# Two linear-attention blocks on one core: the denominators of six units summed through memory on VectorE

## The chip, the cores and the metric

The kernel runs on one core of a Trainium2 chip. The metric is device time in microseconds, the median of several executions. TensorE (PE) multiplies matrices, VectorE (DVE) and ScalarE (ACT) work elementwise, GpSimd (POOL) and SyncE (SP) issue most DMAs. Each engine works through its own instructions in program order and waits on semaphores for the others.

## The reference

Two independent blocks A and B, each with its own input and weights, and their outputs side by side. One block, with S = 2048 tokens, D = 640, 32 heads of 20:

```python
qkv = (x @ wqkv) -> q, k, v per head
phi = lambda t: where(t > 0, t + 1, exp(t)) + 1e-6
pq, pk = phi(q), phi(k)
kv  = einsum("bhsd,bhse->bhde", pk, v)
z   = einsum("bhsd->bhd", pk)
num = einsum("bhqd,bhde->bhqe", pq, kv)
den = einsum("bhqd,bhd->bhq", pq, z)[..., None] + 1e-6
o   = num / den
return concat_heads(o) @ wo
```

## The kernel before

All data is float32; matrices are multiplied as a high and a low half (three products each: high by high, high by low, low by high), rounded by ScalarE with the rest taken by VectorE.

The first half, up to about 290 us, projects the keys of both blocks, applies phi and gathers the products of phi(k) with the input. Its instructions are ordered by a planner (classes Plan and Job, method emit): each piece of work is noted with an engine, a cost and what it reads and writes, and the planner emits them engine by engine by their due times.

The second half has its order written out by hand. The queries are worked on in 8 units of 512 tokens, 0 to 3 of A and 4 to 7 of B. Features are laid out with the head in the fastest place, so that each of the five chunks of 128 partitions holds 4 dimensions of all 32 heads, and a partition belongs to head (partition mod 32). For each unit u there is

- a projection "q" (qmm, lines 890 to 892): five chunks c of 15 matmuls of 512 columns, going through five blocks k of the input, each block as a rounded high half xqh and a low half xql; then phi (qphi, lines 1058 to 1060), and the sum over chunks of phi(q) times z into a tile acc (qacc, lines 1068 and 1070), which holds for each of 128 partitions a partial denominator: four partitions per head still have to be added;
- an output stage "o" (outmm, line 1169): 14 steps, 7 products for each of two halves of the tokens, into the banks pa, pe and psb, evicted by ScalarE (line 1184) and VectorE (line 1185).

The output stage of a unit comes one projection late: q(u), then o(u - 1), then q(u + 1). Smaller work is hung into slots: ("q", u, c, k) is run after block k of chunk c of the projection, ("o", u, s) after step s of the output stage, and what hangs in one slot is issued in the order in which it was put there (functions at and run). A low half is issued on VectorE at the next slot or by flush. Of interest here, for unit v, with w = v - 1:

- load_xraw(v + 1, c) in q(v), chunk 3, and load_xq(v + 1, c) in q(v), chunk 4: the loads (SyncE) of the next unit's input, tile xqs (line 921) and its stored low half xql (line 925);
- round_xq(v + 1, c) in o(w), steps 4, 6, 8, 10 and 12: the five roundings on ScalarE (line 928) that the projection q(v + 1) needs one after the other;
- load_w of B's query weights in q(3), and split_w of them in o(2), steps 1, 3, 5, 7 and 9 (tiles wst, wh, wl); loads of the output stage's forms (form_load, line 1034) in o(3) and after; form_split and form_store, which make B's forms;
- the chain of unit v, in o(w) and on: split_acc makes a high and a low half of acc, denmm multiplies each with a matrix "same" of zeros and ones that adds the four partitions of a head and leaves the sum in all four (bank psd, lines 1080 and 1081), recip (line 1086) inverts in two halves, divide (line 1092) multiplies phi(q) with the inverse, and then d_sums, a_split and d_split make the operands of o(v).

The stage buffers (tag wst, 7 of them) are shared by turns among xqs, the weight loads and the sums of the forms; a load on SyncE waits until the turn's earlier user is done, and so does all that stands behind it on SyncE.

## Time and profile before

| | |
|---|---|
| median of 3 runs | 574.31 us (573.58 to 575.03) |
| profiled execution | 573.32 us |
| its span | 571.5 us |
| TensorE busy | 567.1 us, 99% |
| VectorE, ScalarE, GpSimd busy | 431.0, 341.7, 57.2 us |
| chain that ended last: TensorE, DMA, ScalarE, VectorE | 95%, 2%, 2%, 1% |
| output stages o(0) to o(6) begin at | 335.89, 369.37, 402.73, 436.09, 469.45, 502.81, 536.17 us |

The span is the profile's, from the first to the last instruction of the program. Matmuls overlap in TensorE, so that a group's mean duration is longer than the time that it adds; the chain counts that time.

### The profile page before, as it was taken

To read this page: it belongs to the slowest core of one execution; us is meant where nothing else is said; L and a number is where in the kernel's file an instruction comes from. 1 tells how busy PE (TensorE), PEld (TensorE's weight loads), DVE (VectorE), ACT (ScalarE), POOL (GpSimd) and SP (SyncE) were. 2 spreads that over 40 slices of the span, in tenths; PEclk is the share of its full clock that TensorE was granted. 3 is DMA by queue.
4 is the path that set the end of the run, shared out by engine and by line. 5 is a ranking of instruction groups with operands and counts; after the bars stand their busy time and mean duration, and the time that the engine had idled before them with its cause. 6 is when DMAs were issued, how large, how long until landed. Compare 5 with 4: busy or idle time off the path is not lost.

```text
span 571.5 us, 9524 instructions
## 1 busy us (share of the span) xinstructions
PE 567.1 (99%) x3544; PEld 537.5 (94%) x3544; DVE 431.0 (75%) x700; ACT 341.7 (60%) x619; POOL 57.2 (10%) x93
## 2 busy tenths in 40 slices
PE   9999999999999999999999999999999999999997
PEld 7999999999999999999998899898989989898997
DVE  6888687599887887976355699967788786758792
ACT  6877566673787767655246665746556464644541
POOL 0210011110010011110000103120012201001010
PEclk9999999999999999999999999999999999999999
DMA  8994765748858999686987986662363996122022
GB/s 294 391 249 126 178 168 138 207 139 253 265 152 228 273 293 265 192 250 201 248 243 242 335 275 219 232 211 106 115 232 134 349 391 241 46 75 93 0 93 93
DMA packets 68002, 117.61 MB, mean 206 GB/s; under 512 B 6516, under 2 KB 29812, under 8 KB 67956
## 3 DMA queue, kind: packets, MB, share of 16 engines
q1 hardware_dynamic: 59060, 89.94, 48.4%
q0 software_dynamic: 8608, 26.88, 16.9%
q8 instruction: 28, 0.46, 0.3%
q10 hardware_dynamic: 288, 0.20, 0.1%
q14 instruction: 18, 0.15, 0.1%
HBM read 71.11 MB, written 35.39 MB: 186 GB/s over the span
## 4 chain that ended last, share of the span: by engine, by line
PE 95%; DMA 2%; ACT 2%; DVE 1%; issue 0%; ACTq 0%; DVEq 0%
PE psg L299 23%; PE pa L1169 12%; PE ka L299 9%; PE psq L890 8%; PE psq L892 8%; PE psq L891 8%; PE pe L1169 6%; PE ke L299 5%; PE psk L689 4%; PE psb L1169 4%; PE kb L299 3%; DMA md<-mev 1%; PE pskv L537 1%; PE pskv L950 1%; DMA xj<-in_A_xt 1%; PE psm L564 1%
## 5 line engine op out<-in xcount | busy, mean ns | idle before, releaser
L299 PE MATMUL psg<-pkh,xnh 128*128 128x320 f32 x320 | 99.0, 309 | 0.0
L299 PE MATMUL psg<-pkl,xnh 128*128 128x320 f32 x320 | 98.8, 309 | 0.0
L299 PE MATMUL psg<-pkh,xnl 128*128 128x320 f32 x320 | 98.7, 308 | 0.0
L890 PE MATMUL psq<-xqh,wh 128*128 128x512 f32 x200 | 78.7, 393 | 0.0
L892 PE MATMUL psq<-xqh,wl 128*128 128x512 f32 x200 | 78.1, 391 | 0.0
L891 PE MATMUL psq<-xql,wh 128*128 128x512 f32 x200 | 77.9, 390 | 0.0
L299 PEld LDWEIGHTS psg<-pkl,xnh 128*128 128x128 f32 x320 | 60.1, 188 | 0.0
L299 PEld LDWEIGHTS psg<-pkh,xnl 128*128 128x128 f32 x320 | 60.1, 188 | 0.0
L299 PEld LDWEIGHTS psg<-pkh,xnh 128*128 128x128 f32 x320 | 60.0, 188 | 0.0
L470 ACT ACTIVATE kt<-ka 128x320 f32<-128x320 f32 x52 | 22.7, 437 | 53.6 <-PE ka L299 51.3
L1184 ACT ACTIVATE o<-pa 128x320 f32<-128x320 f32 x64 | 27.9, 438 | 44.8 <-PE pa L1169 44.6
L1060 DVE SCALAR_TENSOR_TENSOR pq<-eq,rq 128x512 f32<-128x512 f32 x40 | 27.6, 691 | 30.8 <-ACT rq L1059 29.9
L387 POOL DMA_DIRECT2D zacc<-ek x32 | 26.4, 832 | 243.7 <-DVE ek L480 187.8
L518 DVE TENSOR_TENSOR gacc<-psg,gacc 128x320 f32<-128x320 f32 x60 | 29.2, 489 | 28.0 <-PE psg L299 27.1
L1058 ACT ACTIVATE eq<-psq 128x512 f32<-128x512 f32 x40 | 23.9, 598 | 36.6 <-PE psq L892 34.2
L892 PEld LDWEIGHTS psq<-xqh,wl 128*128 128x128 f32 x200 | 37.5, 188 | 8.0
L891 PEld LDWEIGHTS psq<-xql,wh 128*128 128x128 f32 x200 | 37.6, 188 | 7.3
L890 PEld LDWEIGHTS psq<-xqh,wh 128*128 128x128 f32 x200 | 37.6, 188 | 7.2
L382 ACT ACTIVATE pkh<-ek,epst 128x640 fp32r<-128x640 f32 x32 | 26.5, 829 | 7.9 <-DVE ek L480 7.7
L1169 PE MATMUL pa<-fh,dah 128*128 128x320 f32 x96 | 29.7, 309 | 0.0
L1169 PE MATMUL pa<-fl,dah 128*128 128x320 f32 x96 | 29.6, 309 | 0.0
L1169 PE MATMUL pa<-fh,dal 128*128 128x320 f32 x96 | 29.6, 308 | 0.0
(212 smaller groups left out, 1553.8 us busy)
## 6 DMA issues: line engine op xcount, KB each, us to landing
zacc<-ek POOLq DMA_DIRECT2D x32, 320.0 KB, 5.7
xql<-xd SPq DMA_DIRECT2D x40, 256.0 KB, 4.6
xd<-xl SPq DMA_DIRECT2D x29, 320.0 KB, 5.1
out<-o POOLq DMA_DIRECT2D x28, 320.0 KB, 3.4
xns<-in_A_x SPq DMA_DIRECT2D x16, 320.0 KB, 4.7
xts<-in_B_xt_tiles SPq DMA_DIRECT2D x16, 320.0 KB, 4.6
xns<-in_B_x SPq DMA_DIRECT2D x16, 320.0 KB, 6.7
xqs<-in_A_xt SPq DMA_DIRECT2D x20, 256.0 KB, 4.9
```

What stands on the lines that cost most here:

```text
L299: nc.tensor.matmul(o, a.r, w.r, start=start and k == i == 0, stop=k == n - 1 and i == 2, skip_group_check=True)
L382: note("ACT", n + 110, lambda: act(hi.r, p.f, AF.Identity, bias=epst), [hi], [p, K0.all], by=8.0)
L387: note("POOL", 1.0, lambda: nc.gpsimd.dma_start(z.f, p.f, **kw), [z], [p], dma=1.0 if first else 1.86)
L518: tt(o, BK[k].tile[:, :HF], o, op=OP.add)
L689: nc.tensor.matmul(o[h][:, :HF], x[a].r, w[c][h * HF:h * HF + HF].r, start=c == 0 and i == 0, stop=c == NC - 1 and i == 2, skip_group_chec ...
L890: nc.tensor.matmul(o, whi, xhi, start=first, stop=False)
L891: nc.tensor.matmul(o, whi, xlo, start=False, stop=False)
L892: nc.tensor.matmul(o, wlo, xhi, start=False, stop=last)
L1058: nc.scalar.activation(e, ps, AF.Exp)
L1060: nc.vector.scalar_tensor_tensor(pq[u][:, c, :], e, 1.0, r, op0=OP.min, op1=OP.add)
L1169: nc.tensor.matmul(ps, x, y, start=start and n == i == 0, stop=n == len(terms) - 1 and i == 2, skip_group_check=True)
L1184: copy = lambda x, y: nc.scalar.activation(x, y, AF.Copy)
```

## The change

For the units 1 to 6 split_acc, denmm and recip are replaced. acc_out writes acc to memory (DRAM) with one DMA from SyncE; acc_turn reads it back with four DMAs, each into 32 partitions, so that the partition is a head and one of four groups of 128 tokens, and the four partial sums lie beside each other in the free dimension; acc_add adds them on VectorE (256 columns, then 128) and inverts 128 columns; spread copies the inverse to the four partitions of each head, 16 copies of 32 partitions by 128 columns, the groups 0 and 1 on ScalarE and 2 and 3 on VectorE. For units 2 to 6 acc_out and acc_turn hang in step 2 of o(v - 1), acc_add and the first spreads in step 9, the others in step 10, the two divisions in 11 and 12; for unit 1 all of these one step later. Units 0 and 7 keep the old chain. The planner gets a further argument, safe, of 0.0 where none is given; no call in the kernel gives one.

```diff
--- before.py
+++ after.py
@@ -83,7 +83,7 @@
         self.jobs = []
         self.pe_at = 0.0
 
-    def note(self, engine, n, fn, w, r, ahead=None, dma=None, late=None, by=None, due=None):
+    def note(self, engine, n, fn, w, r, ahead=None, dma=None, late=None, by=None, due=None, safe=0.0):
         base = self.RATE.get(engine)
         j = Job(engine, base[0] + base[1] * n if base else n, fn, ahead, dma)
         for part, writes in [(p, True) for p in w] + [(p, False) for p in r]:
@@ -106,7 +106,7 @@
         j.late = self.pe_at + (25.0 if late is None else late)
         if by is not None:
             j.late = self.pe_at + by
-        j.by, j.set = by, due
+        j.by, j.set, j.safe = by, due, safe
         self.jobs.append(j)
         return j
 
@@ -150,9 +150,21 @@
                     if e == "HOST":
                         if any(d.done is None for d in j.deps):
                             continue
-                    elif any(d.done is None or d.done + (LAG if d.engine != e or d.dma else 0) > now + 1e-9
-                             for d in j.deps):
-                        continue
+                    else:
+                        at = 0.0
+                        for d in j.deps:
+                            if d.done is None:
+                                at = None
+                                break
+                            t = d.done + (LAG if d.engine != e or d.dma else 0)
+                            if d.dma and j.safe:
+                                t += max(0.0, min(j.safe, j.due - t))
+                            at = max(at, t)
+                        if at is None:
+                            continue
+                        if at > now + 1e-9:
+                            events.add(at)
+                            continue
                     if j.ahead is not None and e != "PE" and j.due - j.ahead > now:
                         events.add(j.due - j.ahead)
                         continue
@@ -1034,6 +1046,7 @@
             nc.sync.dma_start(f32(t)[:, cs], d)
 
     pq, acc, den, dd = {}, {}, {}, {}
+    ad = {u: dram.tile([P, 512], F32, name=f"ad{u}") for u in range(1, NU - 1)}
 
     def qmm(u, c):
         b = u // NG
@@ -1080,6 +1093,36 @@
         nc.tensor.matmul(ps, same, t[:, 0], start=True, stop=False)
         nc.tensor.matmul(ps, same, t[:, 1], start=False, stop=True)
         den[u] = (ps, q2[0].tile([P, 512], F32, name="rd", tag="rd", bufs=1))
+
+    def acc_out(u):
+        nc.sync.dma_start(ad[u], acc[u])
+        den[u] = (None, q2[0].tile([P, 512], F32, name="rd", tag="rd", bufs=1))
+
+    def acc_turn(u):
+
+        v = ad[u].rearrange("(k h) (q j) -> q h k j", k=4, q=4)
+        for q in range(4):
+            nc.sync.dma_start(acc[u][q * H:q * H + H].rearrange("p (k j) -> p k j", k=4), v[q])
+
+    def acc_add(u):
+        t = acc[u]
+        nc.vector.tensor_tensor(t[:, :256], t[:, :256], t[:, 256:], op=OP.add)
+        nc.vector.tensor_tensor(t[:, :P], t[:, :P], t[:, P:256], op=OP.add)
+        nc.vector.reciprocal(t[:, :P], t[:, :P])
+
+    def spread(u, g, copy):
+
+        t = acc[u][g * H:g * H + H, :P]
+        for k in range(4):
+            copy(den[u][1][k * H:k * H + H, g * P:g * P + P], t)
+        if g == 3:
+            acc.pop(u)
+
+    def spread_a(u, g):
+        spread(u, g, lambda y, x: nc.scalar.activation(y, x, AF.Copy))
+
+    def spread_v(u, g):
+        spread(u, g, nc.vector.tensor_copy)
 
     def recip(u, h):
         ps, r = den[u]
@@ -1288,18 +1331,15 @@
                         (("o", v, 0), a_split, v, 0, 1), (("o", w, 13), d_sums, v, 0, 1),
                         (("o", v, 0), d_split, v, 0, 1), (("o", v, 2), d_sums, v, 1, 1),
                         (("o", v, 2), a_split, v, 1, 1), (("o", v, 3), d_split, v, 1, 1)]
-        elif v == 1:
-            chain[v] = [(("o", w, 4), split_acc, v), (("o", w, 7), denmm, v), (("o", w, 8), recip, v, 0),
-                        (("o", w, 10), recip, v, 1), (("o", w, 11), divide, v, 0),
-                         (("o", w, 12), divide, v, 1), (("q", u, 0, 2), d_sums, v, 0), (("q", u, 0, 4), a_split, v, 0),
-                         (("q", u, 1, 2), d_sums, v, 1), (("q", u, 2, 1), d_split, v, 0), (("q", u, 3, 1), a_split, v, 1),
-                         (("q", u, 3, 4), d_split, v, 1)]
         else:
-            chain[v] = [(("o", w, 2), split_acc, v), (("o", w, 5), denmm, v), (("o", w, 7), recip, v, 0),
-                        (("o", w, 9), recip, v, 1), (("o", w, 11), divide, v, 0),
-                         (("o", w, 12), divide, v, 1), (("q", u, 0, 2), d_sums, v, 0), (("q", u, 0, 4), a_split, v, 0),
-                         (("q", u, 1, 2), d_sums, v, 1), (("q", u, 2, 1), d_split, v, 0), (("q", u, 3, 1), a_split, v, 1),
-                         (("q", u, 3, 4), d_split, v, 1)]
+            o = 1 if v == 1 else 0
+            chain[v] = [(("o", w, 2 + o), acc_out, v), (("o", w, 2 + o), acc_turn, v), (("o", w, 9 + o), acc_add, v),
+                        (("o", w, 9 + o), spread_a, v, 0), (("o", w, 9 + o), spread_v, v, 2),
+                        (("o", w, 10 + o), spread_a, v, 1), (("o", w, 10 + o), spread_v, v, 3),
+                        (("o", w, 11 + o), divide, v, 0), (("o", w, 12 + o), divide, v, 1),
+                        (("q", u, 0, 2), d_sums, v, 0), (("q", u, 0, 4), a_split, v, 0),
+                        (("q", u, 1, 2), d_sums, v, 1), (("q", u, 2, 1), d_split, v, 0), (("q", u, 3, 1), a_split, v, 1),
+                        (("q", u, 3, 4), d_split, v, 1)]
     for v in range(NU):
         for a, f, *x in chain[v]:
             at(a, f, *x)
```

## The prediction

> **What bounds the kernel now.** I read the page first, then the chain that ended last, then the queue that issues the loads, then VectorE and ScalarE in the stages that the change touches. Busy time by engine and the chain, from the page:

> ```profile
> PE 567.1 (99%) x3544; PEld 537.5 (94%) x3544; DVE 431.0 (75%) x700; ACT 341.7 (60%) x619; POOL 57.2 (10%) x93
> PE 95%; DMA 2%; ACT 2%; DVE 1%; issue 0%; ACTq 0%; DVEq 0%
> ```

> TensorE works 99% of the span and is 95% of the chain (its granted clock is 1.00 in the rows by stretch further down). So a matmul taken out is time gained, and any wait put ahead of a matmul is time lost. The chain in order of time (start, length, what) shows two output stages; the first belongs to unit 2 and handles the denominators of unit 3, the second to unit 3 and those of unit 4:

> ```profile
> 402.73 1.76 PE pa L1169 x12
> ...
> 408.01 0.23 PE psd L1080
> 408.24 0.23 PE psd L1081
> 408.48 2.64 PE psb L1169 x18
> ...
> 419.03 0.23 PE psq L890
> ...
> 421.12 0.23 PE psq L890
> 421.80 0.23 PE psq L890
> ...
> 436.09 1.76 PE pa L1169 x12
> ...
> 455.16 0.23 PE psq L890
> ```

> The reader is to see that the pieces touch: no gap stands between the output stage and the projection behind it. I count time within a stage from its first row, T = 402.73 and T = 436.09. The stage with its two psd matmuls lasts 16.3 us.

> The third thing to see is the issue queue of SyncE. It works in program order and often stands at a load whose buffer is not free. Its DMAs in these two stages (start, time until the last of them is issued, count at the end):

> ```profile
> 408.20 0.92 SPq L925 DMA_DIRECT2D xql<-xd  x2
> 411.12 0.59 SPq L910 DMA_DIRECT2D wst<-in_B_wq  x1
> 411.80 1.49 SPq L925 DMA_DIRECT2D xql<-xd  x3
> 413.34 0.90 SPq L910 DMA_DIRECT2D wst<-md  x2
> ...
> 441.39 0.33 SPq L921 DMA_DIRECT2D xqs<-in_B_xt  x1
> 441.81 3.00 SPq L925 DMA_DIRECT2D xql<-xd  x5
> 444.91 0.67 SPq L1034 DMA_DIRECT2D fh<-fdh  x1
> ```

> **What goes.** Six units lose two matmuls of 512 columns, 0.23 us each on the chain: 6 x 2 x 0.23 = 2.8 us, all on the path. Their two weight loads overlap and count nothing. VectorE loses two reciprocals and the low half of a split, ScalarE the high half. Neither engine is the bound, so these are cover and not gain. One PSUM bank is used less, and the two "sr" buffers have one user fewer; no wait in the rows is for either, so I take zero for both. The new argument of the planner has the value 0 everywhere, so the first half of the kernel keeps its order: zero.

> **What comes, by price.** The rows for it, by line (count, busy us, mean ns):

> ```profile
> L1086 DVE RECIPROCAL rd<-psd 128x256 f32<-128x256 f32 x16 | 27.9, 1747 | 0.9 <-PE psd L1081 0.9
> L994 DVE TENSOR_TENSOR t<-wst 128x320 f32<-128x320 f32 x2 | 1.0, 488 | 0.0
> L954 DVE TENSOR_TENSOR kvt<-pskv,mask 120x120 f32<-120x120 f32 (+1 forms) x6 | 1.6, 265 | 2.3 <-PE pskv L950 2.3
> L884 ACT ACTIVATE kvh<-kvt 120x120 fp32r<-120x120 f32 (+1 forms) x6 | 1.7, 290 | 8.2 <-DVE kvt L954 8.2
> out<-o SPq DMA_DIRECT2D x2, 160.0 KB, 1.8
> DMA to landing us min/median/max: 2.6/4.6/6.4
> ```

> On VectorE: an add of 256 columns, between 0.27 and 0.49, say 0.42; one of 128, 0.27; a reciprocal of 128, half of 1.75, 0.88. Together 1.6 us. Four spreading copies per group on VectorE or ScalarE, 0.27 to 0.29 each with their overlap taken off, about 1.0 us a group. Per unit VectorE gives up 2 x 1.75 + 0.7 and takes 1.6 + 2.0: less work. ScalarE takes 2.0 and gives up 0.6; at 60% busy that is hidden if it comes on time.

> The DMAs are what matters: one of 256 KB out, then, only when it has landed, four of 64 KB back, each issued by SyncE in about 0.4 us. No row has 64 KB in blocks of 512 bytes to 32 partitions. Its bounds are the 1.8 us of a 160 KB transfer on an empty queue and the 4.6 us median of 256 KB (the last row above, for xql). I take 1.8, since SyncE has issued nothing else behind the first hop and so the queue has drained. From the landing of the first hop to that of the last return is then 3 x 0.4 + 1.8 = 3.0 us.

> **Where it stands in the queue.** The first hop is noted at step 2 of the output stage, but on SyncE it stands behind everything that the projection before noted: all five xql loads and, in T = 402.73, the last weight load of B. That one (411.12) waits for a buffer that VectorE frees at 411.1, after the psb addition:

> ```profile
> 409.84 0.49 DVE L1185 TENSOR_TENSOR o<-psb,o 128x320 f32<-128x320 f32 x1 [2.05 <-PE psb L1169]
> 410.27 0.82 DVE L881 TENSOR_TENSOR wl<-wst,wh 128x640 fp32r<-128x640 f32 x1
> ...
> 412.48 0.44 ACT L1184 ACTIVATE o<-pa 128x320 f32<-128x320 f32 x1 [2.22 <-PE pa L1169]
> 412.81 0.62 ACT L928 ACTIVATE xqh<-xqs 128x512 fp32r<-128x512 f32 x1
> ```

> So the first hop takes the place of the wst<-md at 413.34, 0.47 earlier by the missing matmuls: 412.9, which is T+10.1. The addition of the quarters is placed at step 9, which ends on TensorE about there. The landings in these places, from the DMA view of each of the two stretches:

> ```profile
> xql<-xd SPq DMA_DIRECT2D x3, 256.0 KB, 4.2
> wst<-md SPq DMA_DIRECT2D x2, 320.0 KB, 4.6
> ...
> xql<-xd SPq DMA_DIRECT2D x5, 256.0 KB, 6.3
> ```

> **Unit 3, step by step.** First hop issued 412.9, landed 4.4 later (between the 4.2 and 4.6 of its neighbours): 417.3. Returns landed 420.4. VectorE adds and inverts until 422.0. ScalarE, which has stood at its first spread since step 9, does four copies, the eviction of step 10 (0.33) and the rounding of the fourth xq block (0.62): 424.0. Then four copies, an eviction, and the fifth block: 426.0. Behind these waits are queued on VectorE the last wl, two divisions and two additions, on ScalarE those two roundings. The last wl comes out at about 424, before TensorE asks for it. TensorE asks for the fifth block at 421.80 - 0.47 = 421.3. It stands 4.7 us, at the fourth block and the fifth.

> **Unit 4.** The xqs load at 441.39 waits for a split on VectorE that comes about 1.3 us sooner, since the two halves of the old split no longer stand ahead of it. The hop takes the place of the fh at 444.91: 443.6. There the queue is full and xql takes 6.3: landed 449.9. Returns 452.9, added 454.6, fifth block rounded 4.0 later, 458.6. TensorE asks at 455.16 - 0.47 = 454.7: it stands 3.9 us. Behind this hop stand the twenty form loads for the next output stage; they start some 7 us later and that stage 3.4 later. The last of them is issued at 463.8 and goes into the sixth product of the stage that begins at 469.45, near 480, so this is covered.

> **The other four** are in time. The rows: the starts of the output stages of units 0, 1 and 4 from the chain, the last addition into the sums of units 1 and 2 from VectorE's timeline, and from SyncE's the last form load and the loads ahead of unit 5's hop.

> ```profile
> 335.89 1.76 PE pa L1169 x12
> ...
> 369.37 1.76 PE pa L1169 x12
> ...
> 469.45 1.76 PE pa L1169 x12
> ```

> ```profile
> 341.46 0.75 DVE L1070 SCALAR_TENSOR_TENSOR acc<-pq,z,acc 128x512 f32<-128x512 f32 x1
> 371.50 0.75 DVE L1070 SCALAR_TENSOR_TENSOR acc<-pq,z,acc 128x512 f32<-128x512 f32 x1
> ```

> ```profile
> 463.82 0.42 SPq L1034 DMA_DIRECT2D fl<-fdl  x1
> ...
> 468.76 2.61 SPq L925 DMA_DIRECT2D xql<-xd  x5
> ```

> The fifth block is asked for at T+18.6 (421.3 - 402.73), so the last return is due at 18.6 - 4.0 - 1.6 = T+13.0. In unit 2 the sums are ready at 372.25, T+2.9, with SyncE free: at most 2.9 + 4.6 + 3.0 = T+10.5, and I put unit 6 with it. Unit 5's loads have left SyncE by 471.4, T+1.9, so its hop too goes at T+2.9; the queue ahead is full, T+10.7. Unit 1, placed one step later, has its sums at 342.2, T+6.3; with the 2.6 us of a quiet queue and 3.0 it lands near T+12.0, against a deadline of T+13.9, because the fourth rounding stands ahead of its spread. A stall here would have no cover and count whole. The divisions come 2 to 3 us later everywhere; their products are wanted a whole projection later.

> **Sum.** -2.8 + 4.7 + 3.9 = +5.8 us. The profiled run took 573.32 (span 571.5), 1.0 below the median of 574.31; on the median the sum gives 580.1.

> **Rivals.**
> A. The first hop lands at the fastest xql time, 2.6, in both places. Unit 3 stalls 4.7 - 1.8 = 2.9, unit 4 3.9 - 3.7 = 0.2: +0.3, 574.6, no change. Against it: in the stretches concerned nothing landed so fast, and the DMA engines are nearly full:

> ```profile
> 412.50:418.00 5.50, 5.50 (x40) 5.50 (x39) 5.50 (x7) 3.80 (x8) 1.08 (x2) 1.00 0.95 331
> 441.00:451.00 10.00, 10.00 (x69) 9.91 (x68) 6.72 (x9) 5.03 (x11) 2.96 (x6) 1.00 0.85 277
> ```

> (DMA share is the last number but one: 0.95 and 0.85.) [...] The 4.2 to 6.3 us in these places speak against it here.
> B. The returns are slow, 4.6 each: 2.8 more in units 3 and 4, and past the deadlines by 0.9, 0.3, 0.5 and 0.3 in units 1, 2, 5 and 6: +13.4, 587.7. Only the missing row speaks for it.
> C. Faster: no stall, all 2.8 kept, 571.5. It needs the returns by T+13.0 in units 3 and 4 too, so the first hop issued by T+5.6 (4.4 and 3.0 ahead of it). It decides if SyncE is past its loads by then. Against it: 411.12 and 441.39 are waits for VectorE in this very stage, and the five xql follow them.

> **How the numbers follow.** The forecast, with its own range 577 to 584, gets 0.62; A 0.14, B and what lies between 0.12, C 0.09, beyond all 0.03. The range 573 to 588 leaves out C and the rest, 0.12. A measurement can tell about 0.3% (1.7 us) from no change. Faster 0.10 (C and the edge of A), same 0.10, slower 0.80.

> **What would show it.** In the changed profile psd should be left with 4 matmuls. Gaps on TensorE ahead of the fourth and fifth group of the first projection after the output stages of units 2 and 3, and nowhere else; VectorE idle ahead of its first addition in these two, released by the return DMAs; the first hop issued near T+10.1 and T+7.5 there and near T+3 in units 2 and 6. The prediction is wrong if these hops are issued earlier, land in under 3 us, or if gaps open in other units.

## The result and the profile after

The change made the kernel slower: 589.33 us median against 574.67 (the three runs of the table above and a fourth, 575.16), a ratio of 1.0259 (95% interval 1.0243 to 1.0274). The profiled run took 589.36, its span 587.6. The page of the changed kernel, busy times, granted clock in 40 slices, and the chain that ended last:

```profile
PE 571.8 (97%) x3532; PEld 539.5 (92%) x3532; DVE 428.2 (73%) x748; ACT 352.2 (60%) x661; POOL 57.3 (10%) x93
PEclk9999999999999999999999999999979989999999
PE 83%; DMA 7%; ACT 3%; issue 3%; DVE 3%; SPq 1%; DVEq 0%; POOL 0%; ACTq 0%; POOLq 0%
```

TensorE issues twelve matmuls less and is busy 4.7 us longer. A sixth of the chain no longer lies on it, and two slices have lost clock. What remains of psd, by tile, and what TensorE waited for in the whole run (total us, times, longest):

```profile
L1093 PE MATMUL psd<-ac,same x2: 389/394/398, 322.5 to 555.9; 128*128 128x512 f32 x2
```

```profile
PE psq L902 <- ACT xqh L940: 10.3, 4, 5.0
```

Line numbers have moved: 890 to 892 are now 902 to 904, 928 is 940. All waits of note are for the rounded input block, four of them, as the prediction placed them. The stretches from the end of the output stages of units 2 and 3 show what they cost: projection, output stage, projection (length, busy time by engine, granted clock, DMA share, GB/s), first the same two projections in the kernel before, then the three stretches in the changed kernel.

```profile
418.87:435.93 17.06, 17.06 (x78) 14.08 (x76) 15.17 (x24) 10.42 (x16) 2.70 (x5) 1.00 0.44 162
452.23:469.29 17.06, 17.06 (x78) 14.08 (x76) 13.10 (x18) 9.17 (x14) 1.07 (x2) 1.00 1.04 397
```

```profile
418.69:445.06 26.37, 20.65 (x78) 15.98 (x77) 21.62 (x37) 14.77 (x28) 3.77 (x7) 0.81 0.45 152
445.06:460.91 15.85, 15.85 (x110) 15.85 (x108) 6.17 (x10) 6.07 (x13) 2.70 (x5) 1.00 0.67 225
460.91:485.72 24.81, 20.22 (x77) 15.82 (x76) 18.72 (x31) 13.52 (x26) 2.16 (x4) 0.86 0.99 358
```

A projection took 17.06 us before and takes 17.06 after the other units. Here two of them take 26.37 and 24.81, together 17.1 more. TensorE is idle for 5.72 and 4.59 of that (length less busy time, 10.3). But its busy time is up as well, by 3.6 and 3.2 us for the same matmuls. That second part shows in the clock, in two stretches that begin during the waits and run on behind them:

```profile
423.05:433.29 10.24, 6.63 (x15) 4.76 (x16) 8.91 (x18) 6.52 (x16) 2.16 (x4) 0.50 0.62 210
467.43:474.25 6.82, 5.54 (x13) 4.38 (x14) 6.27 (x8) 3.77 (x7) 1.62 (x3) 0.50 1.03 385
```

The granted clock is 0.50 for 10.24 and for 6.82 us. In unit 4's projection it fell during the first of two waits, 4.95 and 0.76 us. In unit 5's it fell during the second of two, 3.14 and 1.45 us, with three matmuls between them:

```profile
466.30 0.50 PE L902 MATMUL psq<-xqh,wh 128*128 128x512 f32 x1 [3.14 <-ACT xqh L940]
468.71 0.79 PE L902 MATMUL psq<-xqh,wh 128*128 128x512 f32 x1 [1.45 <-ACT xqh L940]
```

The chain through unit 3, in order of time (start, length, what):

```profile
413.61 4.84 DMA ad<-acc
418.46 0.32 SPq L1105
...
419.77 1.94 DMA acc<-ad
421.83 0.44 DVE acc L1109
...
422.62 0.96 DVE acc L1111
423.60 0.31 ACT rd L1122
...
425.33 0.52 ACT xqh L940
...
427.63 0.64 ACT xqh L940
428.31 0.80 PE psq L902
429.11 0.43 PE psq L903
...
433.63 0.23 PE psq L902
```

It reads as the prediction's steps: a late first hop, four returns, the additions, the spreads with a rounding between them and another behind, and only then TensorE's fifth block. New are the last three rows: a matmul of 512 columns that adds 0.23 us adds 0.43 for 5 us after the wait.

The account of the span: six output stages shorter by 0.45 (16.30 to 15.85, the first 0.56), -2.8; the two projections, +17.1; the first projection begins at 290.80 and not 289.65, +1.2, in a part whose instructions are the same (in the other runs it began between 289.4 and 292.0); the last stretch, +0.5. Together +16.0, from 571.5 to 587.6.

### The profile page after: what moved, and what is told of

Read it like the earlier page. It is cut to its first block, busy times and chain, and to the rows that moved or that the text cites. A ratio compares the mean times of both kernels' runs of the same rounds, so it can differ in the third digit from the quotient of the medians.

```text
span 587.6 us, 9650 instructions
## 1 busy us (share of the span) xinstructions
PE 571.8 (97%) x3532; PEld 539.5 (92%) x3532; DVE 428.2 (73%) x748; ACT 352.2 (60%) x661; POOL 57.3 (10%) x93
## 4 chain that ended last, share of the span: by engine, by line
PE 83%; DMA 7%; ACT 3%; issue 3%; DVE 3%; SPq 1%; DVEq 0%; POOL 0%; ACTq 0%; POOLq 0%
PE psg L311 18%; PE pa L1212 10%; PE psq L902 8%; PE psq L903 8%; PE psq L904 8%; PE ka L311 8%; PE pe L1212 5%; PE psk L701 4%; PE ke L311 4%; PE psb L1212 3%; DMA md<-mev 2%; PE kb L311 2%; DMA ad<-acc 2%; DMA zacc<-ek 1%; PE pskv L549 1%
## 5 line engine op out<-in xcount | busy, mean ns | idle before, releaser
L902 PE MATMUL psq<-xqh,wh 128*128 128x512 f32 x200 | 81.6, 408 | 10.3 <-ACT xqh L940 10.3
L903 PE MATMUL psq<-xql,wh 128*128 128x512 f32 x200 | 80.2, 401 | 0.0
L904 PE MATMUL psq<-xqh,wl 128*128 128x512 f32 x200 | 80.1, 401 | 0.0
L902 PEld LDWEIGHTS psq<-xqh,wh 128*128 128x128 f32 x200 | 38.9, 195 | 19.9 <-ACT xqh L940 12.3
L1227 ACT ACTIVATE o<-pa 128x320 f32<-128x320 f32 x64 | 27.9, 439 | 43.8 <-PE pa L1212 43.4
L399 POOL DMA_DIRECT2D zacc<-ek x32 | 26.4, 836 | 244.3 <-DVE ek L492 188.5
L530 DVE TENSOR_TENSOR gacc<-psg,gacc 128x320 f32<-128x320 f32 x60 | 29.2, 489 | 26.4 <-PE psg L311 25.5
L904 PEld LDWEIGHTS psq<-xqh,wl 128*128 128x128 f32 x200 | 38.8, 194 | 8.5
L903 PEld LDWEIGHTS psq<-xql,wh 128*128 128x128 f32 x200 | 39.0, 195 | 7.9 <-DMA xql<-xd 0.4
L1135 DVE SCALAR_TENSOR_TENSOR pq<-pq,rd 128x1280 f32<-128x1280 f32 x16 | 23.6, 1482 | 8.4 <-ACT rd L1122 8.3
L1122 ACT ACTIVATE rd<-acc 32x128 f32<-32x128 f32 x48 | 14.8, 308 | 24.8 <-DVE acc L1111 22.0
## 6 DMA issues: line engine op xcount, KB each, us to landing
xql<-xd SPq DMA_DIRECT2D x40, 256.0 KB, 4.4
xqs<-in_A_xt SPq DMA_DIRECT2D x20, 256.0 KB, 5.3
```

The lines of the kernel that those rows point to most:

```text
L399: note("POOL", 1.0, lambda: nc.gpsimd.dma_start(z.f, p.f, **kw), [z], [p], dma=1.0 if first else 1.86)
L530: tt(o, BK[k].tile[:, :HF], o, op=OP.add)
L902: nc.tensor.matmul(o, whi, xhi, start=first, stop=False)
L903: nc.tensor.matmul(o, whi, xlo, start=False, stop=False)
L904: nc.tensor.matmul(o, wlo, xhi, start=False, stop=last)
L1135: nc.vector.scalar_tensor_tensor(p, p, EPS, r, op0=OP.add, op1=OP.mult)
```

## The experiments

The theory: in units 3 and 4 alone the hop is late by its place in SyncE's queue; the fourth and fifth roundings stand behind the spreads; TensorE waits and then runs at half clock; all else is hidden. The rivals: a price in every changed unit; slow matmuls from something other than idleness; the DMA engines as the bound, whichever queue issues.

**Old chain in units 3 and 4.**

```diff
+    NEW = (1, 2, 5, 6)
+        elif v not in NEW:
+            ... (the lines of the chain before)
         else:
```

> Units 3 and 4 keep the old chain through TensorE; units 1, 2, 5 and 6 have the new one. Theory (the loss sits in units 3 and 4 alone: waits of 6.3 and 4.9 us and 5.9 us of matmuls at half clock behind them; each unit that does not wait gains 0.45): 4 x 0.45 = 1.8 us faster than before, the projections behind the output stages of units 2 and 3 back at 17.06 us. Rival (each changed unit pays for the copies and the five DMAs somewhere): slower than before, by about two thirds of the measured loss, +10.

573.36 against 574.16, ratio 0.9979 (0.9966 to 0.9992); every projection from unit 2 on takes 17.06 to 17.17 us, the four changed stages 15.85 to 15.92. So the loss sits in the two units, and the others' stages are shorter by what two matmuls take. Of the 1.8 us expected the medians show 0.8; the interval reaches from 0.5 to 2.0, so it holds the 1.8 but does not single it out. This is the fastest version found; the one without the hop, below, leaves sums out.

**Units 3 and 4 one at a time.** The same edit with (3,) and with (4,).

> The new chain in unit 3 alone. Theory (each unit's loss is its own): the projection behind its output stage as long as in the changed kernel, 26.4 us, with a half clock of 7 to 10 us in it; about +8.8 on before. Rival (units 1 and 2 contribute to it by what they leave behind on the queues): below 25 us.

> The new chain in unit 4 alone. In the changed kernel this unit's projection took 24.8 us behind a late unit 3, with the full clock before it 25.0. Theory (its loss does not need unit 3's): 24 to 25 us, +7 on before. Rival (the loss in unit 4 is a consequence of unit 3's lateness): below 21 us.

Single runs: 583.83 and 582.93, against 574.28 for the kernel before. The projection behind the changed unit, in the one and in the other:

```profile
419.21:446.26 27.05, 21.14 (x77) 16.31 (x76) 22.07 (x37) 14.77 (x28) 3.78 (x7) 0.81 0.44 148
```

```profile
454.14:478.43 24.29, 20.15 (x77) 15.65 (x76) 18.72 (x31) 13.54 (x26) 2.16 (x4) 0.86 1.00 365
```

10.0 and 7.2 us above 17.06, 17.2 together against the 17.1 of both at once. Neither loss needs the other.

**Without the hop.** The five DMAs of each unit are left out, so each sum covers values of one partition and not a head's four.

```diff
-        nc.sync.dma_start(ad[u], acc[u])
...
-            chain[v] = [(("o", w, 2 + o), acc_out, v), (("o", w, 2 + o), acc_turn, v), (("o", w, 9 + o), acc_add, v),
+            chain[v] = [(("o", w, 2 + o), acc_out, v), (("o", w, 9 + o), acc_add, v),
```

> The changed kernel without the DMA out and the four back: the additions work on the partial sums where they lie, so what is summed is not a head's four partitions. The additions, the reciprocal and the 16 copies of each unit stay. Theory (the work on VectorE and ScalarE is hidden, the hop alone costs): all 6 x 0.45 = 2.7 us faster than before. Rival (the copies on ScalarE ahead of the roundings cost by themselves): waits at the fourth or fifth block in every unit, same as before or slower.

571.82 against 573.69, ratio 0.9959 (0.9942 to 0.9976), about 2 us faster; no wait on TensorE behind the first half. The additions, the reciprocals and the 16 copies are hidden. So it is the hop, and what comes late by it, that costs.

**TensorE kept busy while it waits.**

```diff
+    FILL = {(4, 3): 20, (4, 4): 4, (5, 3): 13, (5, 4): 6}
...
+            if c == 0 and (u, k) in FILL:
+                z = bank("psd", "small", 1)
+                for _ in range(FILL[u, k]):
+                    nc.tensor.matmul(z, same, xt[u, 0][0], start=True, stop=True)
```

> The changed kernel, with matmuls of no use put on TensorE ahead of the fourth and fifth block of the projections of units 4 and 5, 20 and 4, then 13 and 6, each 512 columns at 0.23 us, to fill 9.9 of the 11.2 us of waiting. Their sums go to a bank that nobody reads. Theory (the slow matmuls come from TensorE's standing still): granted clock 1.00 throughout, the waits as long as before, and 5.9 us less than the changed kernel, about +9 on before. Rival (the matmuls are slow because of the DMA traffic of these stretches or operands that come late): no change against the changed kernel, +15, or more by the filling. [...]

586.84, ratio 1.0214 (1.0194 to 1.0235). In unit 4's projection the clock stayed at full and the projection took 23.44 us and not 26.37. In unit 5's the wait had become longer: some 3 us were unfilled, the clock fell to half for 3.4 us (mean clock of the run 0.997), and the projection took 26.30. So more was filled there (20 and 6, 25 and 6):

> The kernel with the filling matmuls, filled further where the clock still fell: 20 and 6 in unit 4's projection, 25 and 6 in unit 5's, since the wait there had grown to some 6.1 us with 3.1 unfilled. Theory (idleness lowers the clock): granted clock 1.00 throughout, a further 1.5 to 3 us off the kernel with less filling, +9 to +11 on before, and what is left over before is the waits themselves. Rival (the slow matmuls of unit 5's projection come from the DMA traffic there): they stay, +12 or more.

586.16, ratio 1.0204 (1.0177 to 1.0231). The two projections:

```profile
417.27:440.42 23.15, 23.15 (x103) 18.95 (x102) 19.48 (x33) 14.43 (x28) 3.25 (x6) 1.00 0.46 149
456.27:481.30 25.03, 24.87 (x108) 19.74 (x107) 18.48 (x31) 13.43 (x26) 2.17 (x4) 1.00 0.91 329
```

The clock is 1.00, at about the GB/s of the same projections in the changed kernel (149 and 329 against 152 and 358). That settles the cause of the slow matmuls: idleness, not traffic. But the time is some 12 us above before, where the rival's number lay, and only 3 of the 6.75 us come back (the two projections together take 48.2 us and not 51.2). Unit 4's projection ends sooner, and unit 5's waits longer for it: 25.03 - 17.06 = 8.0 us, where it was 7.75 with half clock. With its matmuls faster, TensorE arrives earlier at a hop that does not: the last xqs load ahead of unit 4's hop goes out 6.0 us after the output stage's start (446.39, stage from 440.42) and not 3.9 (448.96, from 445.06), as VectorE is still working off the chain of unit 3. So the theory's 9 to 11 us was too good by about one; what is left are the waits, set by VectorE and the hop.

**Roundings ahead of the spreads.**

```diff
+    LATE = (3, 4)
...
+            if v in LATE:
+                chain[v] += [(("q", u, 0, 2), acc_add, v), (("q", u, 0, 3), spread_a, v, 0), (("q", u, 0, 3), spread_v, v, 2),
+                             (("q", u, 0, 4), spread_a, v, 1), (("q", u, 0, 4), spread_v, v, 3),
+                             (("q", u, 1, 0), divide, v, 0), (("q", u, 1, 2), divide, v, 1),
+                             (("q", u, 1, 3), d_sums, v, 0), (("q", u, 2, 0), a_split, v, 0),
...
```

> The changed kernel, with the additions, the spreads and the divisions of units 3 and 4 hung later, in the first chunks of the next projection, so that the five roundings stand ahead of the spreads on ScalarE. The DMAs stay where they are. Theory (TensorE waits only because the fourth and fifth rounding stand behind the spread): no waits, all 6 x 0.45 = 2.7 us gained, about -2.7 on before. Rival (the late hop itself delays loads that TensorE needs, or the late divisions make a new wait in front of the output stages of units 3 and 4): +2 to +8.

584.71, ratio 1.0178 (1.0159 to 1.0196). The rival came true. The waits ahead of the projections are gone (17.17 and 17.06 us), and TensorE waits a stage later, for the operands of the output stages of units 3 and 4:

```profile
PE pe L1212 <- DVE dsl L893: 3.5, 2, 2.4
PE pa L1212 <- ACT o L1227: 2.4, 2, 1.6
PE pa L1212 <- DVE dal L893: 2.0, 1, 2.0
```

These stages take 24.51 and 18.98 us and not 15.85, the first with half clock in it (granted clock 0.86 over the stage). The first of the d_sums of unit 3 start 1.6 us ahead of the output stage that needs the operands (434.23, stage from 435.80); in the kernel before they start 15.3 ahead (420.64, stage from 435.93). Hung later, the chain is late at its other end.

**The hop on GpSimd's queue.**

```diff
-        nc.sync.dma_start(ad[u], acc[u])
+        nc.gpsimd.dma_start(ad[u], acc[u])
...
-            nc.sync.dma_start(acc[u][q * H:q * H + H] ...
+            nc.gpsimd.dma_start(acc[u][q * H:q * H + H] ...
```

> The changed kernel, with the five DMAs of each unit issued by GpSimd and not by SyncE. Theory (the hop is late because of its place in SyncE's queue): in units 3 and 4 the first hop is issued within 1 us of the sums, T+3 to T+4, the returns land by T+13, no waits, about -2.7 on before. Rival (the DMA engines are full in these stretches, whoever issues): the returns land after T+15 in one or both, with a wait of 2 us or more and half clock behind it, +2 to +10.

585.60, ratio 1.0201 (1.0176 to 1.0226). GpSimd's timeline in the output stages of units 2 (from 406.33) and 3 (from 439.96), which hold the hops of units 3 and 4:

```profile
409.42 0.54 POOL L1098 DMA_DIRECT2D ad<-acc  x1 [14.12 <-DVE acc L1083]
412.12 2.20 POOL L1105 DMA_DIRECT2D acc<-ad  x4 [2.16 <-DMA ad<-acc]
```

```profile
445.58 0.54 POOL L1098 DMA_DIRECT2D ad<-acc  x1 [0.85 <-DVE acc L1083]
448.46 2.19 POOL L1105 DMA_DIRECT2D acc<-ad  x4 [2.34 <-DMA ad<-acc]
```

In unit 3 the first hop goes out 3.1 us after the stage's start and VectorE adds at 419.0, 12.7 after it and not 19.0; the projection takes 17.78 us, so its place in the queue was most of its trouble. In unit 4 the hop goes out at 5.6, when VectorE has just finished the sums, which come later here, as the row shows; it has landed 2.6 later, but VectorE adds only at 457.2, 17.2 after the start, as late as on SyncE, and the projection takes 25.16 us. There the returns come after T+15, as the rival had it, and they are what is slow now: issued until 450.65, they land in 6.6 us and not 1.9. From the issue of the first return to the addition, units 1 to 4 take 5.4, 4.6, 6.9 and 8.7 us on GpSimd's queue, and 3.9, 3.4, 3.4 and 3.3 on SyncE's. So units 1 and 2, which were in time on SyncE, lose 2.0 and 2.5 us as well. How much of that is GpSimd's way of issuing and how much the traffic is not shown.

**The hop ahead of the loads, on SyncE.**

```diff
-            at(("q", u, 4, c), load_xq, u + 1, c)
+            at(("o", u - 1, 3) if u in (3, 4) else ("q", u, 4, c), load_xq, u + 1, c)
...
-        at(("q", h, c, 2), load_w, "q", 1, c)
+        at(("q", h, c, 2) if c < 4 else ("o", h - 1, 4), load_w, "q", 1, c)
```

> The changed kernel, with the loads that stood ahead of the hops of units 3 and 4 on SyncE put behind them: the five xql loads of units 4 and 5 in step 3 of the output stage, and B's last weight load in step 4. All else stays on SyncE. Theory (place in the queue, and the traffic that goes with it, makes the late hop): first hops issued by T+5.5, returns by T+13, waits of at most 0.6 us, so -2 to -2.7 on before. Rival (the loads are only exchanged for the hop: xql now lands after T+16, where the next projection needs it): waits of 1 us or more on xql in one or both, and with 3 us or more of it the half clock again, +1 to +8.

584.45, ratio 1.0179 (1.0155 to 1.0202). SyncE and ScalarE in the output stage of unit 2, from 403.05:

```profile
408.07 0.42 SPq L1098 DMA_DIRECT2D ad<-acc  x1
412.06 1.75 SPq L1105 DMA_DIRECT2D acc<-ad  x4
...
416.27 0.38 SPq L922 DMA_DIRECT2D wst<-in_B_wq  x1
```

```profile
421.07 0.74 ACT L896 ACTIVATE wh<-wst 128x640 fp32r<-128x640 f32 x1 [6.83 <-DMA wst<-in_B_wq]
421.72 1.25 ACT L1122 ACTIVATE rd<-acc 32x128 f32<-32x128 f32 x4
```

The hop goes out at T+5.0, as expected, but now the displaced weight load is late, and ScalarE stands 6.8 us for it ahead of the same spreads: the projection takes 23.73 us. In unit 4 the projection takes 18.20 and not 24.81, so there the order was worth 6.6 us; then the chain of unit 5, which had been in time, is late in turn, and the projection behind it takes 22.27. The rival was right that loads and hop only change places, though it was not xql that came late.

**Five units changed.** Unit 3 on GpSimd with the later slots of unit 1, unit 4 with the old chain.

```diff
+    NEW = (1, 2, 3, 5, 6)
...
+            o = 1 if v in (1, 3) else 0
...
+        (nc.gpsimd if u == 3 else nc.sync).dma_start(ad[u], acc[u])
```

> The new chain in units 1, 2, 3, 5 and 6 and the old one in unit 4. Unit 3's five DMAs are issued by GpSimd, and its additions and spreads hang one step later, as unit 1's do, so that the fourth rounding stands ahead of them. Theory (in unit 3 the place in SyncE's queue made the loss; with GpSimd the first hop went out at T+3 and the returns were there at T+12.6, before the deadline of T+13.9): no wait anywhere, 5 x 0.45 = 2.2 us faster than before. Rival (GpSimd's DMAs push the loads of unit 4 back): a wait of 1 us or more ahead of unit 4's projection, same as before.

577.60, ratio 1.0055 (1.0035 to 1.0074), slower, where 2.2 us of gain were expected. ScalarE in that stage:

```profile
416.53 0.74 ACT L896 ACTIVATE wh<-wst 128x640 fp32r<-128x640 f32 x1 [2.22 <-DMA wst<-in_B_wq]
...
419.81 1.27 ACT L1122 ACTIVATE rd<-acc 32x128 f32<-32x128 f32 x4 [1.70 <-DVE acc L1111]
```

B's last weight load, with the returns on their way beside it, lands later than before (ScalarE stands 2.22 us for it, and 0.88 in the kernel before); VectorE's low half of it stands ahead of the additions. Unit 4's projection takes 19.01 us, and the next output stage 18.14, since the old chain of unit 4 now meets engines that are behind (TensorE waits 1.1 us for the high half of the sums from ScalarE). The theory was too narrow here: the place in the queue is not all, a hop that goes out early can delay another load of its stage.

## Why the prediction was right and wrong

The sign, the mechanism and the places were right: two units, the fourth and fifth block, the hop behind SyncE's loads, the other four in time, 0.45 us of gain per unit. The size was wrong: +5.8 was forecast, 14.7 measured, beyond the range's 588.0.

The step that failed is the price of a stall. The prediction let TensorE stand 4.7 and 3.9 us and took just these from the time ("A stall here would have no cover and count whole", said of unit 1, is as far as it went). The two terms measured 9.3 and 7.75. Of these 8.45 us too few, 6.75 are matmuls at half clock behind the waits, which the sum did not have, and 1.7 are idle time, 5.72 and 4.59 where 4.7 and 3.9 stood. The second half of the trace of before held no wait to learn this from. Its first microseconds held a hint, where ten matmuls of 512 columns take 4.16 us, and those of the projections add 0.23 us each (TensorE's timeline in the kernel before: start, length, line, operation, tile):

```profile
0.99 4.16 PE L617 MATMUL psi<-idle 128*128 128x512 bf16 x10 [0.99 <-DVE ones L307]
```

It is no more than a hint: these matmuls are in bf16, and the profile's row for these microseconds gives a granted clock of 1.00. By the rows of the changed kernel, a further 0.2 us for each matmul of some 5 to 7 us is about 3 us in each projection; with it the sum would have been about +12, and a range moved up with it would have held the result.

The idle time, step by step. Unit 4's hop, from SyncE's timeline (the stage begins at 445.06):

```profile
452.44 0.77 SPq L1098 DMA_DIRECT2D ad<-acc  x1
458.90 1.74 SPq L1105 DMA_DIRECT2D acc<-ad  x4
```

Issued at T+7.4 (forecast 7.5), landed just ahead of T+13.8 (13.8): the reading of the queue was right to 0.1 us. Unit 3's (stage from 402.84) was issued at T+10.8 (10.1), after an xql that took 1.3 us to issue, and landed in 4.8 (4.4). The returns took 3.3 (3.0) from first issue to last landing: the 64 KB to 32 partitions, which no row of before had, land in 1.9, near the 1.8 that was taken, so rival B's slow returns are refuted, though its 587.7 lay nearest: that nearness was chance. The additions took 1.8 (1.6). The group of four copies was under-priced on ScalarE: 1.29 (1.0), twice on the path, since copies of 0.31 us one behind the other overlap by nothing:

```profile
423.60 1.26 ACT L1122 ACTIVATE rd<-acc 32x128 f32<-32x128 f32 x4 [8.39 <-DVE acc L1111]
```

Rival A fell, the first hop of units 3 and 4 landing in 4.8 and 6.4 us and not 2.6: there the 4.2 to 6.3 us of its neighbours in the trace of before were nearer than the fastest landing. In units 1 and 5 the same hop landed in 2.0, and from GpSimd's queue in 2.4 and 2.6 in units 3 and 4, which speaks for what went ahead of it on SyncE, and not its size, as the reason. Rival C fell with it. "Their products are wanted a whole projection later" held for the four units in time, but not as a reserve: with the chain hung later, the output stages in the experiment with the roundings ahead of the spreads were 8.7 and 3.1 us longer, half clock in the first included.

## What to carry to other kernels

On a saturated TensorE price a wait as its length and the slow matmuls behind it: here 10.3 us of idleness took 17. Before a transfer is put into a chain that the bound engine needs, write down what stands ahead of it on its queue and what the DMA engines carry in that stage; moving it to another queue or ahead gained in one unit here (8.6 and 6.6 us) and made others late (units 1 and 2 on GpSimd's queue, unit 5 with the hop first). Where a change helps in some units and hurts in others, as the new chain did in four units out of six, keep it in the ones with room.

## What was not expected of the hardware

```profile
498.50:501.90 3.40, 2.88 (x7) 2.31 (x8) 3.40 (x5) 1.16 (x2) 1.10 (x3) 0.50 0.48 187
```

A reciprocal on VectorE takes 0.95 us for 128 columns and 1.75 for 256, each of 128 partitions. Turning the sums, so that no head's sum is inverted four times over, left one of 0.95 where two of 1.75 stood; the chain lost more to the hop in units 3 and 4.
